# Retention attention and a snake MLP on one core: the v loads of 13 tiles by SyncE, and seven products for two more pairs of tiles

## The chip, the cores and the metric

The kernel runs on one core of one Trainium2 chip. Its time is the device time of one launch in microseconds (us). A profiled execution of the kernel gives the trace; its time is told beside the median of the runs without a profile. The engines are TensorE (PE, with its weight loads as PEld), VectorE (DVE), ScalarE (ACT), GpSimd (POOL) and SyncE (SP). SyncE computes nothing: it issues transfers.

## The reference

Four sequences of 768 tokens with 8 heads of 64 go through a linear attention with a decaying state; the result is the input of an MLP with the activation h + sin(αh)²/α.

```python
for t in range(S):                     # B=4, H=8, S=768, D=64
    state = gamma[None, :, None, None] * state + np.einsum('bhd,bhe->bhde', k[:, :, t], v[:, :, t])
    y[:, :, t] = scale * np.einsum('bhd,bhde->bhe', q[:, :, t], state)
...
h = x @ w_in                           # x: 3072 x 512, w_in: 512 x 2048
s = np.sin(alpha * h)
g = h + s * s / (alpha + 1e-09)
return (g @ w_out).astype(np.float32)  # w_out: 2048 x 512
```

## The kernel before, in words

The 3072 tokens are 24 tiles of 128. The list `order` (called `P` further down) holds them in the order of work: the first tile of each sequence first, then on through the sequences, the last two of them side by side. The attention of a tile needs its q, k and v, a turned copy of q and k (`qkT`: TensorE's or a DMA's transpose, `turn`, issued by SyncE), masked scores, and the state that the tile before it in the sequence left. v is multiplied by a table of decays before use (`scale_v`). All of this is issued in a written order: every engine works through its instructions in the order of the program.

The tiles `wide` asks for are the 13 tiles P[11] to P[23]. Their q, k and v come one sequence at a time (`load_seq`), eight transfers for each of q, k and v (one per head), all issued by GpSimd as bf16. Sequence 1 brings P[11] to P[13], sequence 2 P[14], P[15], P[16], P[18] and P[20], sequence 3 P[17], P[19], P[21], P[22] and P[23], in two parts. An issue can wait until an earlier transfer has landed; `seen` (a copy of one column of a turned tile) makes GpSimd wait for the turn of P[17] before it goes on to load.

The MLP works on ten groups, of 4, then eight times 2, then 4 tiles. `phase(g, ...)` computes the hidden layer of group g: for a group of two tiles in 8 steps of two blocks of 128 hidden units, for the last in 16. A step is a `Slot`: eight matmuls into the bank `ph` (L610), the sine and the square on ScalarE (L613, L618), and VectorE's sum, which writes `gT` (L625). Beside each step stands a share of the w_out product of the group before it: `outs`, for two tiles four matmuls of 512 columns a step (`ff_out`, L634). Attention is put between at places (g, n), group and step: `burst` works one tile at a time in phases 2 to 5, and `pair` two tiles together at (6, 4), (7, 4) and (8, 1). A pair's first scores lie in the bank pair "pa", which VectorE reads to mask (L407) and to keep the state (L568); the ph of the step behind the pair is given that bank too. The second scores lie in "mm" banks, and its output y in "two", until VectorE leaves it (L561).

For the last two groups the w_out product is taken by the seven products of Strassen's method in Winograd's form (`Seven`): a pair of tiles and the halves of w_out make seven products of 8 matmuls of 256 columns each (L756) in place of 32 of 512. Products 3 and 4 take gT as it is; 5 and 2 take the sums "s" of blocks of gT, 7 and 6 the differences "d", 1 the sums "x". `mix_g` makes s, d and x (L710), two blocks of hidden units with their partners at a time: two operations of 512 columns and one of 256. `mix_w` makes the combinations of w_out for products 4, 3, 1, 7 and 6 (L681). `hold` copies the bank b of products 5 and 2, `cross`, `rest` and `main` add up the outputs.

Of the kernel before, what the change touches and what calls it, by code (L numbers as in the profile page):

```python
# [38 lines left out]
def kernel(  # L39
# [91 lines left out]
    def load_seq(bt, names="qkv", part=slice(None), between=None):  # L131
# [8 lines left out]
        fs = slice(2 * (now[0] - cs[0]), 2 * (now[-1] - cs[0]) + 2)  # L140
        for name, src in (("q", q), ("k", k), ("v", v)):
            if name not in names:
                continue
            for n, (b, m, e) in enumerate(heads):
                if n == 3 and between is not None:
                    scale_v(between, nc.gpsimd)
# [1 line left out]
                o = tv[r, fs, at, :] if name == "v" else tqk[r, fs, "qk".index(name), at, :]
                nc.gpsimd.dma_start(out=o, in_=src[bt, head(b, m, e), now[0] * C:(now[-1] + 1) * C, :].rearrange("(f i) d -> i f d", i=64))  # L149
# [35 lines left out]
    def scale_v(j, eng):  # L185
        t, by = raw["v", j], kg
        if wide(j):
            t, by = t.rearrange("i f p d -> i (f p) d"), kgq
        eng.tensor_mul(t, t, by[:, j % NCH, :, None].to_broadcast([128, H, D]))  # L189
# [474 lines left out]
    w_todo = [(n, i) for n in (4, 3, 1, 7, 6) for i in range(2)]  # L664

    def w_homes():
        for _ in range(5):
            yield big.tile([128, 4, NH], BF16, name="w_mix", tag="qkr", bufs=10)
        for pool, tag, n in ((consts, "dec", 2), (big, "qk_seq1", 3)):
            t = pool.tile([128, n, 4, NH], BF16, name="w_mix", tag=tag)  # L670
            for i in range(n):
                yield t[:, i]
    w_home = w_homes()

    def mix_w(eng):

        n, i = w_todo.pop(0)
# [3 lines left out]
        eng.tensor_tensor(w_mix[n, i], w_block(*a, js), w_block(*b, js), op=op)  # L681
# [38 lines left out]
    class Seven:  # L720
# [20 lines left out]
        def right(self, n, j):  # L741
            if n in (5, 2):
                return w_out[:, j + FH * (n == 5), NH * (n == 5):NH * (n == 5) + NH]
            return w_mix[n, j // 4][:, j % 4]
# [402 lines left out]
```

## Time and profile before

| | |
|---|---|
| median of three runs | 205.86 us (205.36 to 206.05) |
| profiled execution | 207.02 us, of which the span 205.2 |
| TensorE busy | 195.2 us (95%) |
| VectorE, ScalarE, GpSimd busy | 161.5, 151.8, 163.2 us |
| phases 6, 7, 8 | start at 122.33, 137.62, 152.92 us, each some 15.3 to 16.8 long |
| last group's hidden layer, and the end | from 169.73, and from 189.8 to 205.2 us |

The span is the time from the first to the last event of the profile. A row of the timeline gives its start, how long it lasted, the engine, line and operation, output and inputs, the number of instructions, and in brackets the idle time ahead of it and what ended it. A row of a group of equal instructions gives count, busy time and the mean in nanoseconds. A row of the table of stretches gives the stretch, its length, the busy time of PE, PEld, DVE, ACT and POOL with their counts, the granted TensorE clock (1.00 is full), and the DMA share and rate. A row of the waits names engine, line, what was waited for, the total, how often, and the longest.

### The profile page before, as it was taken

What the parts mean: (1) busy time and instruction counts of PE and PEld (TensorE: products, weight loads), DVE (VectorE), ACT (ScalarE), POOL (GpSimd) and SP (SyncE); (2) the same over time, 40 slices, a digit from 0 to 9 for tenths busy, and PEclk for the clock granted to TensorE, in tenths of its full rate; (3) what the DMA queues carried; (4) which work ended last, traced back from release to release, by engine and by line L of the source; (5) the groups of instructions that cost most, each with busy time, mean ns of one, the idle gap of its engine ahead of it and who ended that gap; (6) DMA issues with size and microseconds to landing.
All of it is one profiled execution on the core that took longest, in us unless ns stands there. A gap on an engine that the chain in (4) does not pass through costs nothing.

```text
span 205.2 us, 6029 instructions
## 1 busy us (share of the span) xinstructions
PE 195.2 (95%) x2426; PEld 131.4 (64%) x2455; DVE 161.5 (79%) x344; ACT 151.8 (74%) x312; POOL 163.2 (80%) x204
## 2 busy tenths in 40 slices
...
PEclk9999999999999999999999999999999999999998
...
GB/s 133 147 175 192 201 201 176 167 134 106 231 151 188 104 171 194 170 136 150 143 116 117 89 141 117 120 131 104 105 2 107 51 5 51 3 0 51 54 102 102
DMA packets 103580, 24.82 MB, mean 121 GB/s; under 512 B 93392, under 2 KB 101248, under 8 KB 103552
## 3 DMA queue, kind: packets, MB, share of 16 engines
...
## 4 chain that ended last, share of the span: by engine, by line
PE 83%; DMA 7%; POOL 4%; issue 2%; DVE 2%; ACT 1%; POOLq 0%
PE ph L610 37%; PE po L634 28%; DMA qkT<-qkr 4%; PE a L756 3%; DMA qkr<-in_q_dram 3%; PE ab L756 3%; POOL qkr L125 2%; PE b L756 2%; PE py L373 1%; POOL vr L125 1%; PE c L756 1%; PE pt L291 1%; PE pa L388 1%; PE py L437 1%; POOL w_in L161 1%
## 5 line engine op out<-in xcount | busy, mean ns | idle before, releaser
L625 DVE SCALAR_TENSOR_TENSOR gT<-s,rec_alpha,ph 128x256 bf16<-128x256 f32 (+3 forms) x164 | 79.4, 522 | 25.1 <-ACT s L618 24.6
L610 PE MATMUL ph<-xT,w_in 128*128 128x256 bf16 (+3 forms) x653 | 98.0, 291 | 0.3
L613 ACT ACTIVATE s<-ph,alpha_sb 128x256 f32<-128x256 f32 (+3 forms) x164 | 75.9, 505 | 28.1 <-PE ph L610 26.3
L610 PEld LDWEIGHTS <-w_in 128*128 128x128 bf16 x656 | 63.1, 98 | 29.6 <-DVE s_f L568 0.7
L634 PE MATMUL po<-w_out,gT 128*128 128x512 bf16 x264 | 70.3, 379 | 2.3 <-issue 1.9
L618 ACT ACTIVATE s<-s 128x512 f32<-128x512 f32 (+1 forms) x94 | 58.7, 626 | 2.8
L634 PEld LDWEIGHTS <-gT 128*128 128x128 bf16 x288 | 26.4, 98 | 20.8 <-DVE gT L625 0.5
L710 POOL TENSOR_TENSOR g_mix<-gT 128x512 bf16<-128x512 bf16 (+1 forms) x27 | 25.9, 994 | 7.2 <-DVE gT L625 7.2
L149 POOL DMA_DIRECT2D qk_seq<-in_q_dram x32 | 21.5, 712 | 6.6 <-DMA v_seq<-in_v_dram 6.1
L149 POOL DMA_DIRECT2D qk_seq<-in_k_dram x32 | 21.3, 720 | 1.5 <-DMA qk_seq<-in_q_dram 1.4
L149 POOL DMA_DIRECT2D v_seq<-in_v_dram x24 | 16.8, 743 | 0.0
L681 POOL TENSOR_TENSOR w_mix<-w_out 128x1024 bf16<-128x1024 bf16 x7 | 15.2, 2190 | 0.0
L756 PEld LDWEIGHTS <-g_mix 128*128 128x128 bf16 x128 | 11.9, 98 | 3.6
L644 DVE COPY o_sb<-po 128x512 f32<-128x512 f32 x15 | 10.3, 687 | 2.0 <-PE po L634 1.6
L125 POOL DMA_DIRECT2D vr<-in_v_dram x11 | 10.3, 932 | 1.2 <-DMA w_in<-in_moe_w_in_dram 0.7
L189 POOL TENSOR_TENSOR v_seq<-v_seq,kgq 128x512 bf16<-128x512 bf16 x9 | 9.8, 1097 | 1.4 <-DMA v_seq<-in_v_dram 1.4
L407 DVE TENSOR_TENSOR aTw<-pa,maskq 128x768 bf16<-128x768 f32 x10 | 9.5, 954 | 0.0
L495 DVE TENSOR_TENSOR xT<-py,qg 128x512 bf16<-128x512 f32 x13 | 8.9, 683 | 0.5 <-PE py L453 0.5
L869 PE MATMUL spare<-warm 128*128 128x112 bf16 (+1 forms) x52 | 7.9, 325 | 1.4 <-DVE warm L199 1.2
L391 DVE TENSOR_TENSOR aT<-pa,mask 128x1024 bf16<-128x1024 f32 x7 | 8.5, 1219 | 0.4 <-PE pa L388 0.4
L520 ACT CAST s_q<-s_f 128x256 bf16<-128x256 f32 x13 | 5.1, 393 | 2.7 <-DVE s_f L515 2.7
...
## 6 DMA issues: line engine op xcount, KB each, us to landing
...
vr<-in_v_dram POOLq DMA_DIRECT2D x11, 128.0 KB, 5.3
...
qkr<-in_q_dram POOLq DMA_DIRECT2D x7, 128.0 KB, 6.4
qkr<-in_k_dram POOLq DMA_DIRECT2D x7, 128.0 KB, 5.8
...
```

The lines of the kernel that those rows point to most:

```text
L125: nc.gpsimd.dma_start(out=t, in_=chunk_of(src, j))
L149: nc.gpsimd.dma_start(out=o, in_=src[bt, head(b, m, e), now[0] * C:(now[-1] + 1) * C, :].rearrange("(f i) d -> i f d", i=64))
L189: eng.tensor_mul(t, t, by[:, j % NCH, :, None].to_broadcast([128, H, D]))
L610: nc.tensor.matmul(self.ph[:, m, :], w_in[:, i, f * 128:(f + 1) * 128], xT[g][:, i, self.lo:self.hi], start=(m == 0 and i == 0), stop=(i = ...
L613: nc.scalar.activation(out=self.s[:, m, :], in_=self.ph[:, m, :], func=ACTF.Sin, scale=alpha_sb[:, f:f + 1])
L618: nc.scalar.activation(out=self.s, in_=self.s, func=ACTF.Square)
L625: nc.vector.scalar_tensor_tensor(gT[self.g][:, f, self.lo:self.hi], self.s[:, m, :], rec_alpha[:, f:f + 1], self.ph[:, m, :], op0=ALU.mult ...
L634: nc.tensor.matmul(po[g, ts], gT[g][:, f, ts * C:(ts + 1) * C], w_out[:, f, :], start=(f == 0), stop=(f == FF - 1))
L644: nc.vector.tensor_copy(o_sb, po[g, ts])
L681: eng.tensor_tensor(w_mix[n, i], w_block(*a, js), w_block(*b, js), op=op)
L710: eng.tensor_tensor(o, i0, i1, op=op)
L756: nc.tensor.matmul(t, self.left(n, j), r, start=k not in self.begun, stop=(j == FH - 1), skip_group_check=True)
```

## The change

Lines of the changed kernel are 6 to 30 higher than those of the old one (L155 for L149, L197 for L189, L305 for L297, L618 for L610, L687 for L681, L718 for L710, L764 for L756).

- The v of the 13 wide tiles is loaded as float by SyncE into one tile `vf`, three times eight transfers, each sequence's behind a turn. `scale_v` reads `vf` and writes the bf16 tile. `vf` lies where the gT of the first and the last group lie; sequence 3's v takes part of the place that sequence 2's had, so it waits for the scaling of P[14] and P[15].
- The scaling of P[10] to P[14] goes from VectorE to GpSimd, and so do three w_out combinations. There are now ten combinations of 512 columns and five of 1024, where there were ten of 1024.
- Groups 6 and 7 go by seven products too, with a plan of their own for each (`fast_pieces`): group 6's in the steps of phase 7 is M4, M5, M2 with hold, M3 with cross, nothing beside the pair, M7, half of M6 and of M1, and the rest. Their s, d and x are made by GpSimd, in phases 6 and 7. Hold is on ScalarE there.
- Stores of both tiles of a pair are joined in one, but for group 8, and the exit of a pair's second tile comes at step 5 when the group before is one of seven products.

```diff
+        if "v" in names and "vf" not in raw:
+            raw["vf"] = work.tile([128, 16, NP, D], F32, name="vf", tag="gA", bufs=1)
...
+            if name == "v":
+                vf = raw["vf"][:, 6:16] if bt == 2 else raw["vf"][:, 0:nh]
+                for i, c in enumerate(cs):
+                    raw["vf", bt * NCH + c] = vf[:, 2 * i:2 * i + 2]
...
-                o = tv[r, fs, at, :] if name == "v" else tqk[r, fs, "qk".index(name), at, :]
-                nc.gpsimd.dma_start(out=o, in_=src[bt, head(b, m, e), now[0] * C:(now[-1] + 1) * C, :].rearrange("(f i) d -> i f d", i=64))
+                o = vf[r, fs, at, :] if name == "v" else tqk[r, fs, "qk".index(name), at, :]
+                (nc.sync if name == "v" else nc.gpsimd).dma_start(out=o, in_=src[bt, head(b, m, e), now[0] * C:(now[-1] + 1) * C, :].rearrange("(f i) d -> i f d", i=64))
...
         t, by = raw["v", j], kg
+        o = t
         if wide(j):
-            t, by = t.rearrange("i f p d -> i (f p) d"), kgq
-        eng.tensor_mul(t, t, by[:, j % NCH, :, None].to_broadcast([128, H, D]))
+            o, t = (x.rearrange("i f p d -> i (f p) d") for x in (t, raw["vf", j]))
+            by = kgq
+        eng.tensor_mul(o, t, by[:, j % NCH, :, None].to_broadcast([128, H, D]))
...
-                gT[g] = work.tile([128, FF, n], BF16, name="gT", tag="gT", bufs=2)
+                gT[g] = work.tile([128, FF, n], BF16, name="gT", tag="gA" if sizes[g] == 4 else "gT", bufs=1 if sizes[g] == 4 else 2)
...
-    fast = (8, 9)
+    fast = (6, 7, 8, 9)
...
+    w_todo = {"vr": [(n, j, 2) for n in (7, 6) for j in range(0, FH, 2)] + [(1, 4, 2), (1, 6, 2)],
+              "dec": [(4, 0, 4), (4, 4, 4)], "seq": [(3, 0, 4), (3, 4, 4), (1, 0, 4)]}
+    w_home = {}
+
...
-            if self.g < NG - 1:
+            if self.g == NG - 2:
...
+        if g == NG - 3:
+            s = Seven(g, 0, lambda k: psum.tile([128, 2, NH], F32, name=k, tag="mm", bufs=4)[:, slice(0, 2) if k != "c" else 0])
+            parts = [[(4, range(7))], [(4, range(7, FH)), (3, range(6))], [(3, range(6, FH)), (5, range(5))],
+                     [(5, range(5, FH)), (2, range(4))], [(2, range(4, FH)), s.hold], [s.cross, (1, J)], [s.rest, (7, J)],
+                     [(6, J), s.main]]
+            return [s.steps(*p) for p in parts]
+        if g < NG - 3:
+            def between(k):
+                if k == "a":
+                    return psum.tile([128, 2, NH], F32, name=k, tag="mm", bufs=4)
+                return psum.tile([128, 2, 512], F32, name=k, tag="two")[:, 0].rearrange("p (x n) -> p x n", x=2)[:, slice(0, 2) if k == "b" else 0]
+            s = Seven(g, 0, between)
+            parts = [[(4, J)], [(5, J)], [(2, J), s.hold], [(3, J), s.cross], [], [(7, J)], [(6, range(4)), (1, range(4))],
+                     [(1, range(4, FH)), s.rest, (6, range(4, FH)), s.main]]
+            return [s.steps(*p) for p in parts]
         s = Seven(g, 0, banks)
...
+            if g - 1 in fast and n == 5:
+                run(more, "exit1")
...
+    def scaled(*js):
+        return lambda: [scale_v(j, nc.gpsimd) for j in js]
+
+    load_seq(1, "q", between={3: scaled(P[8])})
     load_seq(1, "k")
     load_chunk(P[10], "v")
-    load_seq(1, "v")
-    load_seq(2, "q")
-    load_seq(2, "k")
-    load_seq(2, "v")
-    load_seq(3, "q", slice(0, 2))
-    load_seq(3, "k", slice(0, 2))
-    for j in P[15:17] + P[18:19]:
-        scale_v(j, nc.gpsimd)
...
-    for i, spot in ((19, (6, 2)), (20, (6, 6)), (21, (7, 2)), (22, (7, 6)), (23, (8, 2))):
+    for i, spot in ((19, (6, 2)), (21, (7, 2)), (22, (7, 6)), (23, (8, 2))):
...
     def last_loads():
-        mix_w(nc.gpsimd)
         nc.gpsimd.tensor_copy(seen, st["qkT", P[17]][:, 0, 0:1])
-        load_seq(3, "v")
-        mix_w(nc.gpsimd)
-        mix_w(nc.gpsimd)
-        scale_v(P[17], nc.gpsimd)
-        load_seq(3, "qk", slice(2, None))
+        load_seq(3, "q", slice(2, None))
+        load_seq(3, "k", slice(2, None))
 
     at((5, 5), last_loads)
-    for i, spot in ((9, (2, 3)), (10, (3, 0)), (11, (3, 3)), (12, (3, 7)), (13, (4, 3)), (14, (4, 6))):
...
-    for i, spot in ((9, (2, 3)), (10, (3, 0)), (11, (3, 3)), (12, (3, 7)), (13, (4, 3)), (14, (4, 6))):
+    for i, spot in ((9, (2, 3)),):
...
+    def loads():
+        load_seq(1, "v")
+        turn(P[12])
+        pieces_w(2, "vr")()
+        scale_v(P[10], nc.gpsimd)
+        pieces_w(2, "vr")()
+        load_seq(2, "q")
+        scale_v(P[11], nc.gpsimd)
+        load_seq(2, "k", between={4: scaled(P[12])})
+        scale_v(P[13], nc.gpsimd)
+        load_seq(3, "q", slice(0, 2), between={4: lambda: mix_w(nc.gpsimd, "dec")})
+        mix_w(nc.gpsimd, "dec")
+
...
-    for spot in ((4, 3), (5, 3), (6, 2)):
-        mixes(spot, lambda: mix_w(nc.vector))
-    for spot in ((7, 0), (7, 2), (7, 6), (7, 7)):
-        mixes(spot, lambda: mix_w(nc.gpsimd))
-    for m in range(0, FH, 2):
-        mixes((8, m + 1), lambda m=m: mix_g(8, m, 2, nc.gpsimd))
+    at((3, 6), lambda: load_seq(2, "v"))
+    at((4, 6), lambda: load_seq(3, "v"))
+    for spot, fn in (((3, 6), pieces_w(3, "vr")), ((3, 6), scaled(P[14], P[15])),
+                     ((3, 6), lambda: load_seq(3, "k", slice(0, 2), some=slice(0, 4))), ((3, 6), pieces_w(1, "vr")),
+                     ((3, 6), lambda: load_seq(3, "k", slice(0, 2), some=slice(4, 8))), ((4, 0), scaled(P[16], P[18], P[20])),
+                     ((4, 5), pieces_w(2, "vr")), ((4, 5), pieces_w(3, "seq")), ((5, 3), scaled(P[17]))):
+        mixes(spot, fn)
+    for g in (6, 7, 8):
+        for m in range(0, FH, 2):
+            mixes((g, m + 1), lambda g=g, m=m: mix_g(g, m, 2, nc.gpsimd))
     for m in range(FH):
         mixes((9, 2 * m + 1 if m < 5 else min(15, m + 9)), lambda m=m: mix_g(9, m, 1, nc.gpsimd if m < 5 else nc.vector))
```

The first place is GpSimd's queue behind the load of tile 10's v. Before, eight transfers of each kind follow each other (v_seq_1195, 1224 and 1250 are the v of sequences 1, 2 and 3, qk_seq_1223 and 1249 the q and k of 2 and 3):

```order
L125 DMA vr<-in_v_dram 128x8x64
L149 DMA v_seq_1195<-in_v_dram 64x6x64 x8
L149 DMA qk_seq_1223<-in_q_dram 64x10x64 x8
L149 DMA qk_seq_1223<-in_k_dram 64x10x64 x8
L149 DMA v_seq_1224<-in_v_dram 64x10x64 x8
L149 DMA qk_seq_1249<-in_q_dram 64x4x64 x8
L149 DMA qk_seq_1249<-in_k_dram 64x4x64 x8
L189 TENSOR_TENSOR v_seq_1224<-v_seq_1224,kgq 128x512 x3
L681 TENSOR_TENSOR w_mix<-w_out 128x1024
L1093 COPY seen<-qkT 128x1
```

After (v_seq_1195 and 1359 are the v of sequences 1 and 2, qk_seq_1358 and 1379 the q and k of 2 and 3):

```order
L125 DMA vr<-in_v_dram 128x8x64
L687 TENSOR_TENSOR w_mix<-w_out 128x512 x2
L197 TENSOR_TENSOR vr<-vr,kg 128x512
L687 TENSOR_TENSOR w_mix<-w_out 128x512 x2
L155 DMA qk_seq_1358<-in_q_dram 64x10x64 x8
L197 TENSOR_TENSOR v_seq_1195<-vf,kgq 128x512
L155 DMA qk_seq_1358<-in_k_dram 64x10x64 x4
...
L687 TENSOR_TENSOR w_mix<-w_out 128x512 x3
L197 TENSOR_TENSOR v_seq_1359<-vf,kgq 128x512 x2
L155 DMA qk_seq_1379<-in_k_dram 64x4x64 x4
L687 TENSOR_TENSOR w_mix<-w_out 128x512
L155 DMA qk_seq_1379<-in_k_dram 64x4x64 x4
```

The v transfers have left this queue; scalings and combinations stand between the q and k transfers, and ahead of the second half of k for P[17]. Further down the same queue of the changed kernel, the rows up to the mixing of group 6 (v_seq_1380 and qk_seq_1379 are sequence 3's):

```order
L687 TENSOR_TENSOR w_mix<-w_out 128x512 x2
L687 TENSOR_TENSOR w_mix<-w_out 128x1024 x3
L197 TENSOR_TENSOR v_seq_1380<-vf,kgq 128x512
L1123 COPY seen<-qkT 128x1
L155 DMA qk_seq_1379<-in_q_dram 64x6x64 x8
L155 DMA qk_seq_1379<-in_k_dram 64x6x64 x8
L718 TENSOR_TENSOR g_mix<-gT 128x512 x2
L718 TENSOR_TENSOR g_mix<-gT 128x256
```

The mixing of group 6, which the old kernel does not have, comes behind all loads of sequence 3.

The second place is TensorE's queue behind the pair at (7, 4). Before, the last matmuls of the pair are followed by the w_out product of group 6:

```order
L421 LDWEIGHTS qk_seq_1249
L421 MATMUL pb_3017<-v_seq_1250,qk_seq_1249 64x64
L634 LDWEIGHTS gT
L634 MATMUL po<-w_out,gT 128x512
L634 LDWEIGHTS gT
```

After:

```order
L429 LDWEIGHTS qk_seq_1379
L429 MATMUL pb_3077<-v_seq_1380,qk_seq_1379 64x64
L618 LDWEIGHTS w_in
L618 MATMUL ph<-xT,w_in 128x256
L618 LDWEIGHTS w_in
```

The hidden layer's next step now follows the pair at once; the seventh product comes behind that step. The third place is SyncE's queue in phases 2 to 5 after the change (qk_seq_1194, 1358 and 1379 are the q and k of sequences 1, 2 and 3):

```order
L305 DMA_TRANSPOSE qkT<-qk_seq_1194 128x8x128
L655 DMA out_dram<-o_sb 128x512
L305 DMA_TRANSPOSE qkT<-qk_seq_1358 128x8x128
L155 DMA vf<-in_v_dram 64x10x64 x8
L655 DMA out_dram<-o_sb 128x512
L305 DMA_TRANSPOSE qkT<-qk_seq_1358 128x8x128
L655 DMA out_dram<-o_sb 128x512
L305 DMA_TRANSPOSE qkT<-qk_seq_1358 128x8x128
L155 DMA vf<-in_v_dram 64x10x64 x8
L655 DMA out_dram<-o_sb 128x512
L305 DMA_TRANSPOSE qkT<-qk_seq_1379 128x8x128
```

Before, turns and stores alternate there; now eight v transfers stand behind the turn of P[14] and again behind that of P[16], ahead of a store and of the next turn.

More of the change, by code (lines that the diff above doesn't have):

```diff
@@ L129, in wide, with load_seq @@
         return j >= NCH + 3 and j % NCH > 0
-    def load_seq(bt, names="qkv", part=slice(None), between=None):
+    def load_seq(bt, names="qkv", part=slice(None), between={}, some=slice(None)):
         cs = [c for c in range(NCH) if wide(bt * NCH + c)]
@@ L143, in load_seq @@
                 continue
[L144 to L146 removed]
+            if name == "v":
+                vf = raw["vf"][:, 6:16] if bt == 2 else raw["vf"][:, 0:nh]
+                for i, c in enumerate(cs):
+                    raw["vf", bt * NCH + c] = vf[:, 2 * i:2 * i + 2]
+            for n, (b, m, e) in list(enumerate(heads))[some]:
+                if n in between:
+                    between[n]()
                 r, at = half(b), 2 * m + e
[L148 to L149 removed]
+                o = vf[r, fs, at, :] if name == "v" else tqk[r, fs, "qk".index(name), at, :]
+                (nc.sync if name == "v" else nc.gpsimd).dma_start(out=o, in_=src[bt, head(b, m, e), now[0] * C:(now[-1] + 1) * C, :].rearrange("(f i) d -> i f d", i=64))
         for i, c in enumerate(cs):
@@ L663, with mix_w @@
              6: ((0, 0), (0, 1), ALU.add), 7: ((1, 0), (1, 1), ALU.add)}
[L664 to L677, printed above, removed]
-        a, b, op = W_MIX[n]
-        js = slice(4 * i, 4 * i + 4)
-        w_mix[n, i] = next(w_home)
-        eng.tensor_tensor(w_mix[n, i], w_block(*a, js), w_block(*b, js), op=op)
+    w_todo = {"vr": [(n, j, 2) for n in (7, 6) for j in range(0, FH, 2)] + [(1, 4, 2), (1, 6, 2)],
+              "dec": [(4, 0, 4), (4, 4, 4)], "seq": [(3, 0, 4), (3, 4, 4), (1, 0, 4)]}
+    w_home = {}
+    def mix_w(eng, home):
+        n, i, c = w_todo[home].pop(0)
+        a, b, op = W_MIX[n]
+        if home == "vr":
+            to = big.tile([128, 2, NH], BF16, name="w_mix", tag="vr", bufs=11)
+        else:
+            if home not in w_home:
+                w_home[home] = (consts if home == "dec" else big).tile(
+                    [128, 2 if home == "dec" else 3, 4, NH], BF16, name="w_mix", tag="dec" if home == "dec" else "qk_seq1")
+            to = w_home[home][:, (2 if home == "dec" else 3) - 1 - len(w_todo[home])]
+        eng.tensor_tensor(to, w_block(*a, slice(i, i + c)), w_block(*b, slice(i, i + c)), op=op)
+        for j in range(c):
+            w_mix[n, i + j] = to[:, j]
     def blocks(t, first, *dims):
@@ L743, in right @@
                 return w_out[:, j + FH * (n == 5), NH * (n == 5):NH * (n == 5) + NH]
[L744 removed]
+            return w_mix[n, j]
         def mm(self, n, j, half=None):
```

14 lines of the change are left out of this document (11 added, 3 removed).

## The prediction

> **What bounds the kernel now.** I read the page's busy shares first, then the table of stretches cut where a phase begins, then the chain that ended last, then GpSimd's own timeline, and phase 7 row by row.
>
> ```profile
> PE 195.2 (95%) x2426; PEld 131.4 (64%) x2455; DVE 161.5 (79%) x344; ACT 151.8 (74%) x312; POOL 163.2 (80%) x204
> PEclk9999999999999999999999999999999999999998
> ...
> 122.33:137.62 15.29, 15.19 (x207) 10.36 (x207) 12.90 (x29) 12.18 (x27) 13.88 (x20) 1.00 1.33 123
> 137.62:152.92 15.30, 15.19 (x207) 10.52 (x208) 12.04 (x27) 11.75 (x25) 10.77 (x10) 1.00 0.43 77
> 152.92:169.73 16.81, 16.24 (x254) 11.30 (x256) 12.86 (x27) 12.23 (x27) 11.22 (x11) 1.00 0.24 50
> ```
>
> The three stretches are phases 6, 7 and 8: TensorE works 15.19 of 15.29 us, at the full granted clock, so it is the bound, and only two things move the end: fewer TensorE cycles, or TensorE waiting. GpSimd had 13.88 us of work in phase 6 and 10.77 in phase 7; that spare time is where the change puts its new work.
>
> ```profile
> 142.13 0.86 PE po L634 x4
> 193.99 1.75 PE b L756 x16
> ```
>
> Two rows of the chain price the two ways of doing w_out: four matmuls of 512 columns take 0.86 us (0.2155 each), sixteen of 256 columns 1.75 (0.1094 each).
>
> **The change, part by part.**
>
> *Groups 6 and 7 by seven products.* A pair of tiles took 32 matmuls x 0.2155 = 6.9 us; seven products take 56 x 0.1094 = 6.1. That is -0.8 a group, **-1.6** for two, all on the path.
>
> *What GpSimd must do before that pays.* The second product in phase 7 (M5, step 1) multiplies the sums "s" of group 6, and its seventh and eighth matmuls need the s of the last mixing step. GpSimd works in program order, so everything ahead in its queue counts.
>
> ```profile
> 67.28 0.91 POOL L125 DMA_DIRECT2D vr<-in_v_dram  x1 [0.17 <-issue]
> ...
> 79.24 2.13 POOL L149 DMA_DIRECT2D qk_seq<-in_q_dram  x3 [2.04 <-DMA v_seq<-in_v_dram]
> ...
> 102.61 4.28 POOL L149 DMA_DIRECT2D qk_seq<-in_k_dram  x7 [0.51 <-DMA qk_seq<-in_q_dram]
> 107.25 0.61 POOL L149 DMA_DIRECT2D qk_seq<-in_k_dram  x1 [0.35 <-DMA qk_seq<-in_q_dram]
> 107.88 3.05 POOL L189 TENSOR_TENSOR v_seq<-v_seq,kgq 128x512 bf16<-128x512 bf16 x3
> 110.89 2.12 POOL L681 TENSOR_TENSOR w_mix<-w_out 128x1024 bf16<-128x1024 bf16 x1
> 113.44 0.19 POOL L1093 COPY seen<-qkT 128x1 bf16<-128x1 bf16 x1 [0.43 <-DMA qkT<-qk_seq]
> ...
> 126.06 5.31 POOL L149 DMA_DIRECT2D qk_seq<-in_q_dram  x8
> 131.28 5.35 POOL L149 DMA_DIRECT2D qk_seq<-in_k_dram  x8
> ...
> 148.92 0.61 POOL L577 CAST s_q<-s_f 128x512 bf16<-128x512 f32 x1 [4.54 <-DVE s_f L572]
> ...
> 158.22 2.90 POOL L710 TENSOR_TENSOR g_mix<-gT 128x512 bf16<-128x512 bf16 x3 [3.52 <-DVE gT L625]
> 161.08 1.04 POOL L189 TENSOR_TENSOR v_seq<-v_seq,kgq 128x512 bf16<-128x512 bf16 x1
> ...
> L710 POOL TENSOR_TENSOR g_mix<-gT 128x512 bf16<-128x512 bf16 x18 | 20.4, 1156 | 7.2 <-DVE gT L625 7.2
> ```
>
> Both kernels issue tile 10's v at 67.28 and are free at 68.2. From there the new queue up to that s holds: q and k of sequence 2, 16 issues x 0.71 (2.13 for three) = 11.4; the first q and k part of sequence 3, 16 x 0.62 (the 107.25 row) = 9.9; its second part, from 126.06 to 131.28 and as long again, 10.4; eleven v scalings x 1.0 (3.05 for three) = 11.0; five w_out combinations of 1024 columns x 2.1 = 10.5; ten of 512 columns, half of that each (1.03), 10.3; the small copy and one state cast, 0.8; three mixing steps x 2.86 (158.22 to 161.08) and the first operation of the fourth, 1.15, together 9.7. Sum 74.0, so 142.2 with no wait. The 24 v issues that left are not in it. The float input of the scaling costs nothing more by the cast's row, which reads as many floats in 0.61.
>
> ```profile
> POOL qk_seq L149 <- DMA v_seq<-in_v_dram: 6.1, 4, 2.0
> vr<-in_v_dram POOLq DMA_DIRECT2D x1, 128.0 KB, 3.5
> ```
>
> Waits come on top. The new scaling of tile 10 stands two combinations (2.1 us) behind the issue of its load, which landed 3.5 us after issue: about 0.5 net of issue time. Issues that had to wait until an earlier v load had landed cost 6.1 us; with those loads gone from the queue I take 1.5, for issues that still wait so and for sequence 2's v, which now comes by SyncE. So s is there at 144.2; the ends are 142.2 (none of it) and 146.3 (the old waits by the issues left, 48 of 72: 4.1).
>
> ```profile
> 137.62 1.04 PE L610 MATMUL ph<-xT,w_in 128*128 128x256 bf16 x8
> 138.50 0.87 DVE L625 SCALAR_TENSOR_TENSOR gT<-s,rec_alpha,ph 128x256 bf16<-128x256 f32 x2
> ```
>
> TensorE wants it at 137.62 + 0.87 (ph, to the next row's 138.50) + 0.87 (M4) + 0.15 (below) + 0.87 (the next ph) + 6 x 0.11 = 141.1. So it waits **3.1** us (ends 1.1 and 5.2; 7.2 if the old 6.1 stays whole). Nothing covers it: the next thing in TensorE's queue is step 2's ph, and while TensorE stands, ScalarE and VectorE have nothing to finish. It is paid once: after it GpSimd has a cast, three scalings and four mixing steps left for group 7, 0.6 + 3.1 + 11.5 = 15.2 us from 146.1, and phase 8 asks for its s only in steps 2 and 3, around 162.
>
> *Phase 7's other waits.* The second product's place is one matter; banks are the other.
>
> ```profile
> 140.44 0.84 ACT L613 ACTIVATE s<-ph,alpha_sb 128x256 f32<-128x256 f32 x2 [0.23 <-PE ph L610]
> L765 ACT COPY b_sb<-b 128x512 f32<-128x512 f32 x2 | 1.2, 585 | 5.2 <-PE b L756 5.2
> 146.32 0.96 DVE L407 TENSOR_TENSOR aTw<-pa,maskq 128x768 bf16<-128x768 f32 x1
> 146.84 1.04 PE L634 MATMUL po<-w_out,gT 128*128 128x512 bf16 x3
> 147.19 0.41 DVE L568 TENSOR_TENSOR s_f<-s_f,pa 128x256 f32<-128x256 f32 x1
> 147.71 1.04 PE L610 MATMUL ph<-xT,w_in 128*128 128x256 bf16 x8
> 148.31 0.48 DVE L572 TENSOR_TENSOR s_f<-s_f,pb 128x128 f32<-128x128 f32 x2
> 148.70 1.01 DVE L404 TENSOR_TENSOR aTw<-pb,maskq 128x384 bf16<-128x384 f32 x2
> 149.63 0.68 DVE L561 TENSOR_TENSOR xT<-y,qg 128x512 bf16<-128x512 f32 x1
> ```
>
> M4's last matmul needs the gT that VectorE writes until 138.50 + 0.87 = 139.37, and TensorE is there at 139.26: 0.15 with the handover. The new copy of b (hold) is 0.585 us on ScalarE, which idled 0.23 a slot: it runs 0.35 late, and with it the bank that the pair's second scores need, 0.4. After the pair the old kernel did four w_out matmuls (0.87, from 146.84 to 147.71) while VectorE masked and kept from bank "pa" (until 147.60); step 4 is empty now, and the next ph wants that bank at once: 0.9. M1's bank is free only when VectorE has left y: 147.60 + 0.87 + 0.48 + 1.01 + 2 x 0.68 = 151.3, and TensorE, with ph, M7, ph and half of M6 from 147.7 on, comes at 150.8: 0.4. Together **1.85** (ends: 0, all of it beside something; 3.5, with the whole hold, mask, keep and two exits in the open). *Phase 8* has the same hold on ScalarE: 0.35 less what its other bank order gives, **0.3** (0 to 0.6).
>
> *At nothing.* VectorE loses eight operations of 0.69 us:
>
> ```profile
> 129.08 0.69 DVE L681 TENSOR_TENSOR w_mix<-w_out 128x1024 bf16<-128x1024 bf16 x1
> ```
>
> it was 79% busy and TensorE's stretches show 0.1 us of idle in 15.3, so there is nothing to win there. SyncE's part:
>
> ```profile
> 0.74 0.46 SPq L172 DMA_DIRECT2D o_sb<-in_q_dram  x1
> 92.86 1.97 SPq L297 DMA_TRANSPOSE qkT<-qk_seq  x1
> 109.29 0.23 PE L395 MATMUL pa<-qkT 64*64 64x128 bf16 x4
> 110.36 1.74 SPq L297 DMA_TRANSPOSE qkT<-qk_seq  x1
> 118.02 0.23 PE L395 MATMUL pa<-qkT 64*64 64x128 bf16 x4
> ```
>
> Eight v issues at 0.46 hold its queue 3.7 us three times, each behind a turn. Tile 15's turn (92.86) comes behind those of sequence 2, at 96.6, or near 99 with a wait of 2.0 as GpSimd's longest, and is needed at 109.29: hidden. Sequence 3's v waits in that queue for GpSimd to scale tiles 14 and 15, whose place it takes, and tile 17's turn is behind it. That turn started at 110.36, was seen landed at 113.44 and is needed at 118.02. Its k part ends on GpSimd's new queue at 68.2 + 39.7 (the same prices) + 2.0 = 109.9 instead of 107.9, so it lands near 115.5, hidden by 2.5. Phase 9 and the end keep their products.
>
> **The sum:** -1.6 + 3.1 + 1.85 + 0.3 = +3.65. The profiled execution took 207.02 us (span 205.2 and 1.8 around it), 1.16 above the median 205.86; it becomes 210.7, and against the median **209.5**.
>
> **A rule beside a row.** The 1024-column combination took 0.69 us on VectorE and 2.12 on GpSimd, 3.1 times as long. The Trainium skill (GPSIMD Engine Reference, section 4.1) puts two-input elementwise work on GpSimd at about twice VectorE's time. By that factor the five wide and ten half-wide combinations would cost about 14 instead of 21 us, GpSimd would be in time, and the first rival's 206.4 would follow; the trace does not agree, and the measured number is used.
>
> **The rivals.** *GpSimd is in time, only the bank waits stay:* -1.6 + 1.85 + 0.3 = +0.55, 206.4. For it: the sum misses by 1.1 us of 74 before any wait. Against it: the 6.1 us of waits before.
>
> *Faster:* GpSimd reaches s by 141.1 and the bank waits cost in phase 7 no more than in phase 8: -1.6 + 0.3 + 0.3 = -1.0, 204.9. It decides if the 74.0 us shrink to 72.9 with nothing waited for, 1.5% off my prices. Against it: step 4's bare bank is 0.9 alone.
>
> *Sequence 2's v late:* the scaling of tiles 14 and 15 stands ahead of half of tile 17's k loads. If the SyncE loads hold it up by 5 us, tile 17 lands at 120.5 instead of 118.02, and GpSimd is as late: 209.5 + 2.5 = 212.0. For it: v_seq landings already held GpSimd 2.0 us at a time.
>
> *The clock:* the longest wait of TensorE in its working phases was 1.14 us, and no slice fell below 9 tenths but the last.
>
> ```profile
> 62.30 0.42 PE L388 MATMUL pa<-qkT 64*64 64x128 bf16 x16 [1.14 <-DMA qkT<-qkr]
> ```
>
> A wait of 3.1 is longer than any shown, and if it lowered the clock to half for as long, it would cost 3.1 again: 212.6. The Trainium skill (TensorE: Matmul & The Clock Gate, Part 1, HAM oscillation) says that idle gaps over some 3.4 us bring TensorE back to half clock; no run here shows it.
>
> **How the numbers follow.** My forecast (207.5 to 212.5) has 0.52; GpSimd in time 0.18; faster 0.13; late v 0.11; the clock 0.06. The range 205.0 to 212.2 leaves out about half of the last three and the far tail of the first, 2 in 10. A measurement tells 0.3% here (0.6 us: 205.24 to 206.48 is no change). Faster: the third and a little of the second, 0.14; same: most of the second, 0.12; the rest slower, 0.74.
>
> **What would show it.** In the changed profile: b's first eight matmuls in phase 7 split after six, with a wait on GpSimd's g_mix of about 3 us; a gap of 0.9 us between the pair's last matmul at step 4 and the next ph, released by VectorE; GpSimd without idle time from 68 to 146; tile 17's turn landed before the burst that needs it. I am wrong if GpSimd's s stands ready when M5 begins, or if the issues, with v gone from the queue, run clearly below 0.62 and 0.71 us.

## The result, and the profile after

The changed kernel takes 216.34 us (median of 3 runs, 215.53 to 216.35), the old one 205.69 beside it: a ratio of 1.0504 (95% interval 1.0467 to 1.0542). It is slower, as forecast, but by nearly three times as much: 10.65 us between the medians, where the forecast had 3.65. Some executions are slow ones, over 1.5% above the fastest of the same kernel: medians and ratios from here on leave them out, and the trace of e6, which is of such a one, is read for the places of waits alone. Below two profiled executions are set side by side; they differ by 8.6 us of span (213.8 against 205.2), 2 less than the medians, because the old kernel's was 1.33 above its median and the changed one's 0.81 below.

The page of the changed kernel:

```profile
PE 199.7 (93%) x2503; PEld 137.1 (64%) x2503; DVE 158.2 (74%) x338; ACT 152.7 (71%) x314; POOL 181.2 (85%) x217
PEclk9999999999999999999999859999999999999999
```

GpSimd works 18 us more than before. Two slices in the middle have a lowered clock, which no slice of the old kernel had there. TensorE's timeline shows where it stood still (idle time and releaser in brackets):

```profile
108.83 0.25 PE L403 MATMUL pa<-qkT 64*64 64x128 bf16 x4 [0.36 <-DMA qkT<-qk_seq]
124.01 0.32 PE L403 MATMUL pb<-qkT 64*64 64x128 bf16 x4 [6.19 <-DMA qkT<-qk_seq]
149.75 0.39 PE L764 MATMUL b<-w_out,g_mix 128*128 128x256 bf16 x2 [0.66 <-POOL g_mix L718]
156.59 1.05 PE L618 MATMUL ph<-xT,w_in 128*128 128x256 bf16 x8 [0.71 <-DVE s_f L576]
```

The large one is 6.19 us in burst 16, waiting for the turn of tile 17. The table of stretches is cut at that wait and where phases 6, 7, 8 and 9 begin:

```profile
117.80:124.01 6.21, 0.02 (x4) 0.00 (x0) 0.00 (x0) 0.29 (x1) 6.21 (x5) 0.80 1.07 183
124.01:130.13 6.12, 6.12 (x72) 3.86 (x73) 3.60 (x8) 1.50 (x4) 6.12 (x8) 0.64 0.41 63
130.13:145.47 15.34, 15.34 (x209) 10.52 (x208) 12.75 (x28) 12.34 (x27) 15.34 (x21) 1.00 1.20 117
145.47:162.09 16.62, 15.17 (x234) 12.75 (x233) 12.12 (x28) 12.14 (x26) 14.63 (x17) 1.00 0.38 65
162.09:178.35 16.26, 16.12 (x283) 13.65 (x281) 13.93 (x28) 12.72 (x28) 14.54 (x16) 1.00 0.34 51
```

In the second row TensorE is busy throughout, at a granted clock of 0.64. The same work, from the second scores to the first row of phase 6, took 4.07 us before (118.10 to 122.17) and takes 6.12 now:

```profile
118.10 0.23 PE L395 MATMUL pb<-qkT 64*64 64x128 bf16 x4
122.17 1.04 PE L610 MATMUL ph<-xT,w_in 128*128 128x256 bf16 x8
```

So the 8.6 us are, counted from row to row of the timelines: 0.28 gained before the wait, 6.19 for it, 2.05 for the clock behind it, -0.1 in phase 6 (15.34 against 15.45), +1.3 in phase 7 (16.62 against 15.30), -0.55 in phase 8 (16.26 against 16.81).

Why tile 17 was late stands in two queues, and in the time that its k took to land. SyncE's queue:

```profile
71.33 5.39 SPq L155 DMA_DIRECT2D vf<-in_v_dram  x8
...
94.94 1.23 SPq L305 DMA_TRANSPOSE qkT<-qk_seq  x1
96.23 8.20 SPq L155 DMA_DIRECT2D vf<-in_v_dram  x8
...
105.21 1.33 SPq L305 DMA_TRANSPOSE qkT<-qk_seq  x1
...
109.39 7.39 SPq L155 DMA_DIRECT2D vf<-in_v_dram  x8
116.89 1.23 SPq L655 DMA_DIRECT2D out_dram<-o_sb  x1
120.90 1.28 SPq L305 DMA_TRANSPOSE qkT<-qk_seq  x1
```

Eight v issues hold SyncE for 5.4, 8.2 and 7.4 us, not 3.7. And GpSimd's:

```profile
107.33 2.04 POOL L197 TENSOR_TENSOR v_seq<-vf,kgq 128x512 bf16<-128x512 f32 x2 [4.11 <-DMA out_dram<-o_sb]
109.31 2.50 POOL L155 DMA_DIRECT2D qk_seq<-in_k_dram  x4
111.78 1.21 POOL L687 TENSOR_TENSOR w_mix<-w_out 128x512 bf16<-128x512 bf16 x1
112.89 2.49 POOL L155 DMA_DIRECT2D qk_seq<-in_k_dram  x4
...
145.60 8.65 POOL L718 TENSOR_TENSOR g_mix<-gT 128x512 bf16<-128x512 bf16 x9
```

It stood for 4.11 us ahead of the scaling of tiles 14 and 15. The releaser named is a store, but what that scaling reads is sequence 2's v, whose last issue ended at 104.43. Tile 17's k was out only at 115.38. SyncE was through with sequence 3's v and the store at 118.12, and then waited for the k (its waits from 112 to 125 us):

```profile
SPq L305 <- DMA qk_seq<-in_k_dram: 2.4, 1, 2.4
```

The turn began at 120.90, that is 5.5 us after the last k issue, where the old kernel needed 2.5 (107.86 to 110.36), and TensorE had it at 124.01. The last four k transfers, issued while SyncE issued sequence 3's v, took 5.8 to 6.1 us from issue to landing; the old kernel's eight took 2.6 to 4.8.

### The profile page after: what moved, and what is told of

Its sections match the earlier page's. It is cut to its first block, busy times and chain, and to the rows that moved or that the text cites. A ratio compares the mean times of both kernels' runs of the same rounds, so it can differ in the third digit from the quotient of the medians.

```text
span 213.8 us, 6202 instructions
## 1 busy us (share of the span) xinstructions
PE 199.7 (93%) x2503; PEld 137.1 (64%) x2503; DVE 158.2 (74%) x338; ACT 152.7 (71%) x314; POOL 181.2 (85%) x217
## 4 chain that ended last, share of the span: by engine, by line
PE 58%; POOL 17%; DMA 7%; SPq 7%; DVE 4%; ACT 3%; issue 2%; POOLq 0%; ACTq 0%
PE ph L618 26%; PE po L642 14%; SPq L155 6%; PE a L764 5%; POOL qk_seq L155 5%; POOL g_mix L718 5%; DMA qkr<-in_q_dram 3%; DMA vf<-in_v_dram 3%; PE ab L764 2%; POOL w_mix L687 2%; PE b L764 2%; PE c L764 2%; POOL qkr L125 2%; ACT s L621 1%; DVE gT L633 1%
## 5 line engine op out<-in xcount | busy, mean ns | idle before, releaser
L618 PE MATMUL ph<-xT,w_in 128*128 128x256 bf16 (+3 forms) x656 | 99.1, 292 | 0.8 <-DVE s_f L576 0.7
L618 PEld LDWEIGHTS <-w_in 128*128 128x128 bf16 x656 | 63.6, 99 | 27.8 <-DVE s_f L576 1.1
L642 PE MATMUL po<-w_out,gT 128*128 128x512 bf16 x224 | 59.1, 384 | 0.0
L718 POOL TENSOR_TENSOR g_mix<-gT 128x512 bf16<-128x512 bf16 (+1 forms) x51 | 49.3, 1024 | 5.0 <-DVE gT L633 3.7
L642 PEld LDWEIGHTS <-gT 128*128 128x128 bf16 x224 | 20.6, 98 | 16.8 <-issue 0.6
L764 PEld LDWEIGHTS <-g_mix 128*128 128x128 bf16 x208 | 19.4, 98 | 6.0 <-POOL g_mix L718 0.9
L155 POOL DMA_DIRECT2D qk_seq<-in_q_dram x32 | 21.5, 705 | 1.3 <-DMA vr<-in_v_dram 1.2
L687 POOL TENSOR_TENSOR w_mix<-w_out 128x512 bf16<-128x512 bf16 (+1 forms) x15 | 21.9, 1504 | 0.0
L155 POOL DMA_DIRECT2D qk_seq<-in_k_dram x32 | 21.5, 720 | 0.3 <-issue 0.2
L197 POOL TENSOR_TENSOR v_seq<-vf,kgq 128x512 bf16<-128x512 f32 x13 | 13.8, 1077 | 5.6 <-DMA out_dram<-o_sb 4.1
L764 PEld LDWEIGHTS <-gT 128*128 128x128 bf16 x88 | 7.9, 98 | 2.2 <-DVE gT L633 0.3
L764 PE MATMUL b<-w_out,g_mix 128*128 128x256 bf16 x64 | 8.5, 273 | 0.7 <-POOL g_mix L718 0.7
L652 DVE COPY o_sb<-po 128x512 f32<-128x512 f32 x11 | 7.6, 690 | 2.0 <-PE po L642 1.6
L764 PE MATMUL a<-w_mix,gT 128*128 128x256 bf16 (+1 forms) x72 | 8.7, 261 | 0.0
```

The source lines that it names most:

```text
L155: (nc.sync if name == "v" else nc.gpsimd).dma_start(out=o, in_=src[bt, head(b, m, e), now[0] * C:(now[-1] + 1) * C, :].rearrange("(f i) d ...
L197: eng.tensor_mul(o, t, by[:, j % NCH, :, None].to_broadcast([128, H, D]))
L618: nc.tensor.matmul(self.ph[:, m, :], w_in[:, i, f * 128:(f + 1) * 128], xT[g][:, i, self.lo:self.hi], start=(m == 0 and i == 0), stop=(i = ...
L642: nc.tensor.matmul(po[g, ts], gT[g][:, f, ts * C:(ts + 1) * C], w_out[:, f, :], start=(f == 0), stop=(f == FF - 1))
L687: eng.tensor_tensor(to, w_block(*a, slice(i, i + c)), w_block(*b, slice(i, i + c)), op=op)
L718: eng.tensor_tensor(o, i0, i1, op=op)
```

## The experiments

All start from the changed kernel; each is timed beside the old one, which had medians of 205.99 to 206.47. First the lateness of tile 17.

**e1, sequence 2's v earlier.**

```diff
-    at((3, 6), lambda: load_seq(2, "v"))
+    at((3, 2), lambda: load_seq(2, "v"))
```

> Changed kernel with sequence 2's v issued by SyncE four steps earlier, at (3,2), ahead of tile 14's turn instead of behind it. Theory A (the 4.1 us that GpSimd waited for this v is the source): the wait is gone, tile 17's k is issued by 111.3 instead of 115.4, and tile 17 is turned in time or up to 2.1 us late; the clock is not lowered; 216.3 - 4.1 - 2.2 = 210.0 with 2.1 us late, 207.9 in time. Theory B (GpSimd's queue is too long by itself, the v is not what counts): tile 17's k still ends after 114, the wait at burst 16 stays over 4 us, 213 to 216.

214.92 us, 1.0404 (1.0347 to 1.0462): in theory B's range, but not by its path. SyncE's queue and TensorE's waits:

```profile
82.21 13.74 SPq L155 DMA_DIRECT2D vf<-in_v_dram  x8
...
100.12 1.62 SPq L305 DMA_TRANSPOSE qkT<-qk_seq  x1
```

```profile
105.37 0.32 PE L403 MATMUL pa<-qkT 64*64 64x128 bf16 x4 [4.05 <-DMA qkT<-qk_seq]
148.55 0.39 PE L764 MATMUL b<-w_out,g_mix 128*128 128x256 bf16 x2 [2.03 <-POOL g_mix L718]
```

GpSimd no longer waited for v and there was no wait at burst 16. But beside GpSimd's q and k loads of the same sequence the eight issues took 13.74 us, tile 14's turn stood behind them (94.94 before, 100.12 now), and TensorE waited 4.05 us at burst 14 and 2.03 at M5, with a lowered clock behind each. GpSimd came to the scaling only 1.2 us earlier (106.11 for 107.33), because new waits for q and k stood ahead of it, and k still ended at 114.14; burst 16 did not wait because TensorE itself was that late. So this run does not decide between A and B. It shows that where the v goes in SyncE's queue decides which turn is late.

**e2, k first.**

```diff
-    for spot, fn in (((3, 6), pieces_w(3, "vr")), ((3, 6), scaled(P[14], P[15])),
-                     ((3, 6), lambda: load_seq(3, "k", slice(0, 2), some=slice(0, 4))), ((3, 6), pieces_w(1, "vr")),
-                     ((3, 6), lambda: load_seq(3, "k", slice(0, 2), some=slice(4, 8))), ((4, 0), scaled(P[16], P[18], P[20])),
+    for spot, fn in (((3, 6), lambda: load_seq(3, "k", slice(0, 2))), ((3, 6), pieces_w(3, "vr")), ((3, 6), scaled(P[14], P[15])),
+                     ((3, 6), pieces_w(1, "vr")), ((4, 0), scaled(P[16], P[18], P[20])),
```

> Changed kernel with all eight k transfers of tiles 17 and 19 ahead of the three w_out combinations and of the scaling of tiles 14 and 15 in GpSimd's queue; sequence 2's v stays late. Theory A and B both: k is issued from about 100 to 105, tile 17 is turned by 113, no wait at burst 16 and no lower clock, 207.9; burst 15 may wait up to 0.5 us for tile 14's v. Theory C (transfers in flight together make the k land late: SyncE's v loads share the DMA engines): the time from the last k issue to the start of the turn stays near 5.5 us as in the changed kernel, or more beside sequence 2's v, but there is time for it; then no wait either, and the turn starts near 110.

212.90 us, 1.031 (1.0254 to 1.0366). GpSimd's k, SyncE's queue, TensorE:

```profile
99.31 4.97 POOL L155 DMA_DIRECT2D qk_seq<-in_k_dram  x8
```

```profile
110.16 7.04 SPq L155 DMA_DIRECT2D vf<-in_v_dram  x8
117.31 0.74 SPq L655 DMA_DIRECT2D out_dram<-o_sb  x1
118.87 1.28 SPq L305 DMA_TRANSPOSE qkT<-qk_seq  x1
```

```profile
122.16 0.25 PE L403 MATMUL pb<-qkT 64*64 64x128 bf16 x4 [2.72 <-DMA qkT<-qk_seq]
```

k was out by 104.3, as expected, and had landed by some 110: these transfers took 5.4 to 6.5 us from issue to landing, beside sequence 2's v, which is theory C's sign. Still the turn began at 118.87: it stands behind sequence 3's eight v issues, which waited for the scaling of tiles 14 and 15. I missed that queue in my expectation. The wait at burst 16 fell from 6.19 to 2.72 us.

**e4, both; e5, both with groups 6 and 7 by 512 columns** (`fast = (8, 9)`, no mixing for 6 and 7).

> Both edits: v early and k first. If lateness at burst 16 and the clock that falls with it are all of the 8.4 us, 207.5 to 207.9: the two phases of seven products cost 0.8 us more than before. With GpSimd 4 us earlier its sums for group 6 are ready at 145.6 against 141 wanted on the old time scale, so M5 in phase 7 now waits about 3 to 4.5 us (0.66 in the changed kernel, where TensorE itself was 8 late): then 210.5 to 212.

> Both edits, and groups 6 and 7 by 32 matmuls of 512 columns as before; no mixing for them. What is left is the loads by SyncE and the combinations on GpSimd. If these cost nothing once tile 17 is in time, 205.2 to 205.7 (0.45 us were gained by burst 16 in the changed kernel). If the seven products of groups 6 and 7 pay 1.6 us less the bank waits, it is slower than the kernel with both edits by up to 0.5; if they cost the M5 wait, faster than it by 2 to 6.

214.44 (1.0385, 1.0319 to 1.0451) and 214.92 (1.0401, 1.0342 to 1.046): both have e1's wait at burst 14 (4.48 and 5.25 us, their eight issues 14.51 and 13.87), so they don't tell on the products. With TensorE that late, no difference is seen.

**e6, sequence 3's v behind tile 17's turn, with e2's edit; e7, the same with `fast = (8, 9)`.**

```diff
-    at((4, 6), lambda: load_seq(3, "v"))
+    at((5, 2), lambda: load_seq(3, "v"))
```

> Changed kernel with k first (as in the kernel named k first) and sequence 3's v issued by SyncE behind tile 17's turn instead of ahead of it. Theory D (in the k-first kernel tile 17's k was issued by 104.2, but its turn stood in SyncE's queue behind eight v issues of 7.0 us, which waited for GpSimd's scaling of tiles 14 and 15): the turn starts near 110 and lands by 114, the wait at burst 16 (2.7) and the lower clock behind it are gone. Then GpSimd's sums of group 6, ready near 146 to 147, are next: M5 in phase 7 waits 4 to 6 us, with a lower clock behind it, and the time stays at 211 to 213.5. Rival: the lateness at burst 16 was all that there was; 208. Rival theory C (transfers in flight slow the turn): the turn still starts after 115.

> The same, with groups 6 and 7 by 32 matmuls of 512 columns as before and no mixing for them. If the M5 wait is what holds the kernel with v behind tile 17's turn, this one is 4 to 6 us faster than that, 206 to 207.3 (0.9 us may be left at burst 15, where tile 15's turn stands behind sequence 2's v). If not, it is within 1 us of it.

214.43 (1.0414, 1.035 to 1.0479) and 209.91 (1.0171, 1.0108 to 1.0234). In neither trace is there a wait at burst 16, so theory D on SyncE's queue holds. e6's trace waits at burst 15 (4.17 us) and at M5 (0.94 and 2.45) instead, and the same kernel without the products of groups 6 and 7 is 4.5 us faster: the wait forecast for M5 is there as soon as TensorE is less late. e6 is 0.9 above the range given, e7 2.6; at burst 15, where tile 15's turn stands behind sequence 2's v, e7 lost 1.88 us:

```profile
112.64 0.25 PE L403 MATMUL pa<-qkT 64*64 64x128 bf16 x4 [1.88 <-DMA qkT<-qk_seq]
```

**e8, tiles 10 to 13 scaled by VectorE, on top of e6; e9, the same with `fast = (8, 9)`.**

```diff
-    for i, spot in ((9, (2, 3)),):
+    for i, spot in ((9, (2, 3)), (10, (3, 0)), (11, (3, 3)), (12, (3, 7)), (13, (4, 3))):
```

> The kernel with k first and v behind tile 17's turn, with the scaling of tiles 10 to 13 back on VectorE at the places of the old kernel: GpSimd loses four operations of 1.05 us and its wait of 1.9 for tile 11's v, 6 us. Theory D: its sums of group 6 are ready at 140 to 141.5, M5 waits 0 to 0.5 us, and the kernel comes near the old one: 0.45 gained ahead of phase 5, 1.6 by the products, against 0.7 behind the pair at (7, 4) and up to 0.9 at burst 15: 205.2 to 206.5. If the M5 wait is not GpSimd's queue, it stays where the kernel without this edit is.

> The same with groups 6 and 7 by 512 columns. With GpSimd in time, the difference of these two is what the seven products of groups 6 and 7 are worth: my terms are -1.6 for the columns and about +0.9 for bank waits, so this one is slower by 0.3 to 1.0, at 205.8 to 207. If bank waits eat all of it, the two are within 0.3.

215.43 (1.0441, 1.037 to 1.0512) and 208.97 (1.0123, 1.0046 to 1.0199). Both expectations failed, e8's clearly. TensorE at M5 in e8 (the granted clock was 0.95 throughout that execution, so its matmuls are some per cent longer):

```profile
144.43 0.39 PE L764 MATMUL b<-w_out,g_mix 128*128 128x256 bf16 x2 [0.85 <-POOL g_mix L718]
147.25 0.39 PE L764 MATMUL b<-w_out,g_mix 128*128 128x256 bf16 x2 [2.43 <-POOL g_mix L718]
```

GpSimd's waits in that kernel:

```profile
POOL qk_seq L155 <- DMA qk_seq<-in_k_dram: 3.9, 3, 2.0
POOL qk_seq L155 <- DMA qk_seq<-in_q_dram: 1.6, 3, 0.9
```

With four scalings less, its loads ran ahead of those under way, and 5.5 us of waits for earlier q and k came instead; e6's trace, with the four scalings, has 2.1 us of them, and e2's none. In this stretch GpSimd is held by the transfers as much as by its own work, and taking work from it moves its sums by less than the work taken.

**e11, on top of e8, seven products for groups 7, 8 and 9 but not for 6** (`fast = (7, 8, 9)`).

> The kernel with scalings on VectorE, k first and v behind tile 17's turn, with seven products for groups 7, 8 and 9 (group 6 by 512 columns). GpSimd's mixing of group 7 has a whole phase more, so M5 should not wait. Theory D: the group pays about 0.5 us against the kernel with two groups only: 208.3 to 208.6 where that had 208.97, and far below the 215.4 with group 6 as well. If group 7 costs as much as group 6, about 212.

207.24 (1.0058, 1.0029 to 1.0086), 8.2 below e8 and 1.7 below e9. Group 6's products cost about 8 us; group 7's cost nothing, and may pay (the intervals of e9 and e11 overlap). In the trace GpSimd waits for group 7's gT, 6.97 us, and nothing waits for GpSimd's sums. What is left is a wait at burst 15:

```profile
110.88 0.25 PE L403 MATMUL pa<-qkT 64*64 64x128 bf16 x4 [1.38 <-DMA qkT<-qk_seq]
```

**e12, the products alone: loads and scalings as in the old kernel, five combinations on VectorE; e13, the same with `fast = (7, 8, 9)`.**

```diff
-                (nc.sync if name == "v" else nc.gpsimd).dma_start(out=o, in_=src[bt, head(b, m, e), now[0] * C:(now[-1] + 1) * C, :].rearrange("(f i) d -> i f d", i=64))
+                nc.gpsimd.dma_start(out=o, in_=src[bt, head(b, m, e), now[0] * C:(now[-1] + 1) * C, :].rearrange("(f i) d -> i f d", i=64))
...
+    for spot, n, home in (((4, 3), 1, "dec"), ((4, 5), 1, "dec"), ((5, 3), 1, "seq"), ((6, 2), 1, "seq"), ((6, 7), 1, "seq")):
+        mixes(spot, lambda n=n, home=home: mix_w(nc.vector, home))
```

> The seven products of groups 6 and 7 alone: v as bf16 by GpSimd, scalings and turns at the places of the old kernel, five wide w_out combinations on VectorE, ten narrow on GpSimd. No wait at burst 16. GpSimd's last k load ends near 137, and from there the mixing of group 6 needs 12.5 us with two scalings and a cast: s at 149.6, where M5 wants it at 141.1: a wait of 8.5 and a lower clock behind it (2.2), less 0.6 for the products net of bank waits: 215 to 217. Rival: without SyncE's loads the products just pay; 204.5 to 205.5.

> The same old loads with seven products for groups 7, 8 and 9 only. GpSimd's mixing of group 7 starts behind the last loads and is done by 157, M5 in phase 8 wants it near 158: no wait. Theory D: 0.5 us below the old kernel, at about 205.5 where that has 206.0. If the loads by SyncE are not what costs the kernels with two and three groups their 3 us, this one is at 208 too.

218.95 (1.0611, 1.0545 to 1.0677) and 207.25 (1.0043, 1.0005 to 1.008). e12 at M5:

```profile
144.00 0.39 PE L758 MATMUL b<-w_out,g_mix 128*128 128x256 bf16 x2 [3.31 <-POOL g_mix L712]
147.40 0.61 PE L758 MATMUL b<-w_out,g_mix 128*128 128x256 bf16 x2 [3.01 <-POOL g_mix L712]
151.24 0.61 PE L758 MATMUL b<-w_out,g_mix 128*128 128x256 bf16 x2 [3.23 <-POOL g_mix L712]
```

9.55 us, where 8.5 were expected, once for each of three mixing steps. The granted clock was 0.50 for 10 us behind the first of them, and the time is 2 us above the range. So SyncE's loads did bring GpSimd forward; not by enough for group 6. e13 is not faster than the old kernel: TensorE waits for gT, and so for VectorE, whose five combinations took 6.6 us there (the old kernel's three took 2.1):

```profile
107.82 1.02 PE L636 MATMUL po<-w_out,gT 128*128 128x512 bf16 x4 [0.56 <-DVE gT L627]
...
144.59 1.03 PE L612 MATMUL ph<-xT,w_in 128*128 128x256 bf16 x8 [0.98 <-DVE gT L627]
```

**e10, the clock: 24 matmuls that nobody reads, ahead of burst 16 in the changed kernel.**

```diff
+    def busy():
+        bank = psum.tile([128, 512], F32, name="busy", tag="mm", bufs=4)
+        for _ in range(24):
+            nc.tensor.matmul(bank, w_out[:, 0, 0:128], w_out[:, 0, :], start=True, stop=True)
+
+    atts[5][6].insert(0, busy)
```

> Changed kernel with 24 matmuls of 512 columns that nobody reads (5.2 us at 0.2155) in TensorE's queue ahead of burst 16, where it waited 6.2 us for tile 17. Theory E (the half clock of some 4 us behind that wait comes of the idle array): the wait shrinks to about 1 us, the clock stays whole there, and 2.2 us are saved: 213.3 to 214.5. Rival: the clock falls for another reason at that place; then 216 or more, and the stretch behind the burst still shows about half.

217.39 (1.0504, 1.0433 to 1.0574), not faster: the time lies in the rival's range, the clock behind the burst does not. Its timeline, and its stretches of 2 us (the granted clock is the third number from the end):

```profile
124.86 0.25 PE L403 MATMUL pb<-qkT 64*64 64x128 bf16 x4 [1.17 <-DMA qkT<-qk_seq]
150.32 0.52 PE L764 MATMUL b<-w_out,g_mix 128*128 128x256 bf16 x2 [2.42 <-POOL g_mix L718]
```

```profile
124.00:126.00 2.00, 0.98 (x50) 0.85 (x52) 0.73 (x2) 0.00 (x0) 2.00 (x2) 1.00 1.07 259
126.00:128.00 2.00, 2.00 (x19) 1.59 (x18) 2.00 (x5) 0.59 (x2) 2.00 (x2) 1.00 0.19 35
...
150.00:152.00 2.00, 1.68 (x9) 1.23 (x10) 0.00 (x0) 0.00 (x0) 2.00 (x4) 0.61 0.00 0
152.00:154.00 2.00, 2.00 (x12) 1.43 (x11) 0.00 (x0) 1.38 (x3) 2.00 (x2) 0.53 0.00 0
```

The clock stayed whole behind burst 16, so the idle array was the reason. But the microseconds saved there were lost at M5: TensorE came to it earlier, GpSimd's sums did not, the wait grew from 0.66 to 2.42, and that wait lowered the clock in its turn.

**e14 and e15, sequence 2's v back on GpSimd (with `fast = (7, 8, 9)` and `(8, 9)`, else as e11); e16 and e17, the same with tile 14 scaled by VectorE.**

```diff
-                (nc.sync if name == "v" else nc.gpsimd).dma_start(out=o, in_=src[bt, head(b, m, e), now[0] * C:(now[-1] + 1) * C, :].rearrange("(f i) d -> i f d", i=64))
+                (nc.sync if name == "v" and bt != 2 else nc.gpsimd).dma_start(out=o, in_=src[bt, head(b, m, e), now[0] * C:(now[-1] + 1) * C, :].rearrange("(f i) d -> i f d", i=64))
...
-        load_seq(2, "k", between={4: scaled(P[12])})
+        load_seq(2, "k", between={})
+        load_seq(2, "v")
```

> The kernel with seven products for groups 7, 8 and 9 (scalings on VectorE, k first, sequence 3's v behind tile 17's turn), with sequence 2's v as bf16 by GpSimd behind its k. Theory F (SyncE's eight issues of sequence 2's v ahead of tile 15's turn are what is left): no wait of 0.9 to 1.9 us at burst 15, and 205.2 to 206.2 where that kernel had 207.4 and the old one 206.3. Rival (the rest of the change costs it, or GpSimd's 5.7 us more make tile 17 late): 207 or more.

> The same with seven products for groups 8 and 9 only. If a group by seven products is worth 0.8 us of columns less 0.3 of bank waits, this one is 0.5 slower than its neighbour; if theory F holds it is at 205.7 to 206.7, as the old kernel.

> The kernel with sequence 2's v by GpSimd and seven products for groups 7, 8 and 9, with tile 14's scaling on VectorE at its old place. Theory F: no wait over 1 us behind phase 3, no lower clock, 205.2 to 206.2 where the old kernel has 206.0 to 206.3. Rival: VectorE, which now has six scalings back, makes TensorE wait for its copies and gT as in the kernel of old loads with three groups (0.6 and 1.0 us there): 206.5 to 207.7.

> The same with seven products for groups 8 and 9 only: 0.3 to 0.8 us slower than its neighbour if group 7's products pay as their columns say, within 0.3 if bank waits eat it.

e14 and e15 took 212.31 (1.0285, 1.0242 to 1.0328) and 212.97 (1.029, 1.0242 to 1.0337): tile 15's turn came in time, but the scaling of tile 14 stood behind three combinations.

```profile
113.74 0.43 PE L429 MATMUL pa<-v_seq,qk_seq 64*64 64x64 bf16 x16 [3.19 <-POOL v_seq L197]
```

With that scaling on VectorE, e16 takes 207.12 (1.0026, 0.9994 to 1.0058) and e17 207.85 (1.0059, 1.0023 to 1.0094). In e16 no wait for a turn is left behind phase 3; one at burst 12 and one for VectorE's copy remain:

```profile
86.77 0.25 PE L403 MATMUL pa<-qkT 64*64 64x128 bf16 x4 [1.36 <-DMA qkT<-qk_seq]
...
102.00 1.03 PE L618 MATMUL ph<-xT,w_in 128*128 128x256 bf16 x8 [0.62 <-DVE o_sb L652]
```

So sequence 2's v in SyncE's queue was what cost burst 15: there theory F holds. But the time is in the rival's range, and the wait for VectorE's copy is the rival's; the whole is a draw with the old kernel. Group 7's products are worth 0.7 us in both pairs, by the medians; the intervals overlap in both, so that is the size seen and not one proved. No version beats the old kernel.

These four runs also answer theory C. The eight k transfers that e2 put first took a median of 2.7 to 3.1 us from issue to landing here, where SyncE has no v under way, and 5.6 to 7.0 in e2, e7, e8, e9 and e11, where it issues sequence 2's v at that time. So k lands later beside SyncE's loads; in the changed kernel those were sequence 3's, and no run takes them away alone.

## Why the prediction was right or wrong

- **Direction.** Right, but in part by luck: 8.2 of the 8.6 us are tile 17's wait and the clock behind it, which the sum had at nothing; its own terms, phases 7 and 8, came to some +0.8 in place of 3.65. M5's wait is there once TensorE is less late (e6 against e7, e8, e12).
- **The step that failed: "SyncE's part", under "at nothing".** Eight v issues were taken at 0.46 us, from an issue at the very start of the kernel with nothing else in flight. They took 0.67 (5.39 for eight, transfers of 96 KB) to 1.03 (8.20, 160 KB), and 1.7 beside GpSimd's loads in e1. Tile 17 was to land near 115.5 with 2.5 us to spare; it was waited for until 124.0. Its k issues ended 5.5 us later than worked out (115.38 for 109.9; 4.1 of that is GpSimd's wait for sequence 2's v, for which, with other waits, 1.5 stood in the sum). And the k took 3 us more to land than in the old kernel, whose 2.5 us from the last issue to the turn the prediction had carried over: that SyncE's loads would slow GpSimd's was a term at nothing without a reason. SyncE's queue itself, free at 118.12, was not what the turn waited for last; in e2 it was.
- **The rival "sequence 2's v late"** named the mechanism, the place and the releaser, and was given 0.11 and 2.5 us. It was the main case, with 6.19; the slower landing of the k, 3 us of that, it did not have.
- **The clock rival** was right too, at another place: it was priced at 3.1 us behind M5 with 0.06; it cost 2.05 behind burst 16. The two rivals belonged together: a wait of that length brings the lower clock with it, so that the late v should have been priced at 2.5 plus the clock.
- **M5's wait: 3.1 forecast, about 0.8 measured** (b's first six matmuls and the wait of 0.66 span 1.48 us, of which six at 0.11 are work). This was not a gain: the sums were ready at 149.65 (the start of the last step's first operation, 148.5, and 1.15), 5.4 us later than the 144.2 of the prediction, mostly by that 4.1; TensorE itself was 7.85 late. The two delays overlapped where the sum added them. e8, where TensorE is less late, shows 3.28 (at its clock of 0.95).
- **The products and banks of phases 7 and 8.** Phase 8: -0.55 measured, -0.5 forecast. Phase 7's bank waits: the pair 0.71 for 0.9, M4 0.17 for 0.15, M1 0.2 for 0.4, and none that stands out for the hold, which had 0.4: 1.1 for 1.85.
- **VectorE's relief "at nothing"**: 0.28 us gained by burst 16, near enough; no run shows what gained it.

The Trainium skill (TensorE: Matmul & The Clock Gate, Part 1, HAM oscillation) puts the harm at idle gaps over some 3.4 us. The rows here lower the clock behind 2.72 us (e2, 0.50 in the stretch from 124 to 126), 2.42 us (e10) and 2.03 us (e1), and not behind 1.88 (e7): on this kernel the limit to plan with is 2 us at most. Each of these is one execution; two others of e7, not traced, have a mean clock of 0.992 and 0.990, so 1.9 us may be at the edge already.

Still open: e9 had only 0.97 us of waits for a turn in its trace, at 206.86 us, but a median of 208.97. Its other runs were not traced.
